# The sums of the tokens' quarters move from GpSimd to VectorE, with a new order of the work

## The chip, the cores and the metric

The kernel runs on one core of a Trainium2 chip. A core has five engines that each work through a queue of their own, in order: TensorE (PE in the profile) for matrix products, VectorE (DVE), ScalarE (ACT), GpSimd (POOL) and SyncE (SP), which here only issues DMAs. Semaphores make one engine wait for another. The metric is the device time of one execution in microseconds; the time of a kernel is the median of several runs.

## The reference

The input `x` has 2048 tokens of width 512. After a layer norm two branches read it, and their product is added to `x`:

```python
x = A_x
xn = _layernorm(x, axis=-1)
s = _A_ref(xn, A_wqkv, A_wo)                   # linear attention, 32 heads of 16
g = _silu(_B_ref(xn, B_w1, B_w2, B_w3, B_w4))  # token shift mixer, then an MLP of width 1376
return x + s * g
```

Branch A projects `xn` to q, k and v and applies `phi(t) = where(t > 0, t + 1, exp(t)) + 1e-6` to q and k. It forms `kv = sum over tokens of phi(k) v` per head and `z = sum of phi(k)`, and gives `phi(q) kv / (phi(q) z + 1e-6)`, times `wo`. Branch B norms its input again, multiplies by `w1`, applies gelu, shifts the four quarters of the channels by +1, -1, +2 and -2 tokens, multiplies by `w2` and adds its input; then it norms, multiplies by `w3`, applies gelu, multiplies by `w4` and adds again. All of it is float32.

## The kernel before

**Precision and products.** Each operand of a large matrix product is split into a rounded part and the rest (`rounded`: ScalarE rounds to the high part, VectorE subtracts it to get the low part). `products` then takes three matmuls for each product: high by high, high by low, low by high. Larger products are done as two by two blocks with seven block products in place of eight (the scheme of Strassen in Winograd's form). `seven` does so for the mixer, the MLP and the attention, `keys_queries` for the projections to keys and queries. The operands of those seven products are sums and differences of blocks.

**Stages.** The tokens go in four blocks of 512. In the first 245 us the kernel does, for each block, the keys and queries, the sums over tokens (`gram`, tile `g`), the first half of the mixer (`mix1`, tile `h`, then `forms`) and the second (`mix2`, tiles `pam`, `pbm`, `pem`, output `o`). From 245 us on it does the MLP and the attention block by block (`up_pair`, `down` into `acc`, `attend_pair`, `gate`).

**The step that the change touches.** Blocks 0 and 1 form keys and queries with plain products. Blocks 2 and 3 use seven products, with forms of the weights made once in `forms_kq` (tiles `kq`, asked for by the item `("T",)` of the list `ORD`) and forms of the tokens made in `make_u`. `make_u(b)` first subtracts the token means from four transposed chunks `xt` (128 channels by 512 tokens each) and rounds these to tiles `u`. Then it makes four sums `us_0` to `us_3` of quarters. With quarters numbered by token half and by channel half, they are `q10+q11`, `us_0-q00`, `q00-q10` and `q01-us_1`. Each is two instructions of 128 by 256 elements, on the engine that `SUMS` names, so eight in each block and sixteen in all. ScalarE and VectorE round them to the left operands `s1` to `s4` of `keys_queries` (products into `pbk`, `pek`, `pak`).

**Banks.** Matmul results go to PSUM, where four banks of 512 columns (pool `mm`) are used in turn beside four accumulators. A bank comes free when VectorE or ScalarE has read it: in `mix1` by the product `ht`, in `mix2` by the additions `o`, in `keys_queries` by `p1k`, `p5k` and `u2k`.

**What sets the order.** The program first lists all 5074 operations. `Plan.emit` then puts them into the engines' queues with a planner that holds an estimate of each operation's time. Every operation has a due time, worked out backward from the matmul that needs it; among those that can go at about the same time, the one due first goes. A tile of the pool `p` (96 buffers) may be opened only a certain time ahead of its due time; `SOON` adds to this time for items of `ORD` ("T" for the forms `kq`, "u" for `make_u`). The table `SOONER` holds pairs: the number of an operation in the list, and by how many quarters of a microsecond its due time is made earlier (later if negative). What an operation reads is made due earlier with it. The planner lets a two-operand operation of VectorE on SBUF wait until one of GpSimd has ended (`port`). Since one plan sets all queues, a changed entry can move instructions and DMAs on SP's and POOL's queues too.

Of the kernel before, what the change touches and what calls it, by code (L numbers as in the profile page):

```python
# [396 lines left out]
def linear_attn_gated_by_mixer(  # L397
# [27 lines left out]
    WARM = 8  # L425
    PIECE = BT + W
    EARLY = (), ()
    SUMS = "POOL"
    SOON = {"T": 24.0, "u": 5.0}
    AHEAD = 70.0, 50.0, 30.0, 10.0, 0.0  # L430
    TH = BT // 2
    EDGE = 64
# [15 lines left out]
    def rounds(name):  # L448

        return piece(name + "h", F32R), piece(name + "l", F32R)  # L450
# [221 lines left out]
    def make_u(b):  # L672
# [12 lines left out]
        for n, u, v, op in ((0, q[1, 0], q[1, 1], ALU.add), (1, parts[0], q[0, 0], ALU.subtract),  # L685
                            (2, q[0, 0], q[1, 0], ALU.subtract), (3, q[0, 1], parts[1], ALU.subtract)):
            for c in range(2):
                pl.tt(parts[n][c], u[c], v[c], op, eng=SUMS)
            hl = rounds(f"us{b}_{n}")
# [702 lines left out]
    for what, *args in ORD:  # L1392
        pl.early = SOON.get(what, 0.0)
        DO[what](*args)
# [48 lines left out]
    for b in range(NQ):  # L1443
# [64 lines left out]
                gate(b * QT + QT - 1, a, o, D // 2, late=True, by_dma=False, whole=o > 0)  # L1508

    SOONER = (  # L1510
        23, 66, 83, 70, 97, 31, 156, 19, 186, 1, 424, 8, 536, 32, 925, -16, 930, -96, 981, 8, 1172, 16, 1530, 32,
        1761, 16, 3072, -16, 4805, 8, 4809, 438,
    )
    pl.emit(first=6.0, lead={"p": 14.0, "w": 14.0, "ab": 10.0}, reserve={"p": 20, "w": 1, "ab": 0}, window=12.0,
            ahead=6.0, table=SOONER)
# [37 lines left out]
```

## Time and profile before

| | us |
|---|---|
| median of 3 runs (lowest to highest) | 524.08 (522.8 to 525.65) |
| the profiled execution | 524.87 |
| its span, first to last instruction | 523.2 |
| TensorE busy in it | 511.5 |
| VectorE busy | 417.0 |
| ScalarE busy | 338.9 |
| GpSimd busy | 117.9 |

The profile records one execution. Busy time is time in which an engine has an instruction running; waiting for a semaphore is not counted, but an instruction that has started and is held up by something else counts as busy for all of that. The span does not contain the 1.67 us by which the execution's time is longer. "Granted clock" is the TensorE clock as a share of full speed. In rows of instructions the columns are the start, the duration, the engine, the line, the operation, and output <- inputs by the names of the program with block and chunk numbers partly left out; brackets hold the idle time before and what ended it. Where a row ends in x2, two instructions are drawn together.

### The profile page before, as it was taken

Reading aid. Unit: us, or ns where it says so; the run is one execution under the profiler, and the core shown is the slowest. Engines: PE = TensorE matmul, PEld = TensorE weight load, DVE = VectorE, ACT = ScalarE, POOL = GpSimd, SP = SyncE. Lnnn points to the kernel's source line nnn. Section 1 sums busy time; section 2 is a strip of 40 time slices with the busy share of each in tenths; the row PEclk is TensorE's granted clock in tenths of the full one; section 3 lists DMA queues with packets and bytes.
Section 4 is the critical chain, followed back from the end, with each engine's and each line's share of the span. In section 5 each row is a group of like instructions: output and inputs, shape, how many; then the busy total and the mean of one; then the engine's idle time right before and its main releaser. Section 6 shows DMA issues by size and latency. Waiting matters only on the chain.

```text
span 523.2 us, 8982 instructions
## 1 busy us (share of the span) xinstructions
PE 511.5 (98%) x2983; PEld 444.3 (85%) x2983; DVE 417.0 (80%) x816; ACT 338.9 (65%) x694; POOL 117.9 (23%) x207
## 2 busy tenths in 40 slices
PE   8999999998999899999999999999999999999996
PEld 6777888897778787898989989899899899999985
DVE  4986669999879996789999988786797758755635
ACT  6898777773899589887777744445453456443621
POOL 3488321246622843111100002000020000200000
PEclk9999999998999899999999999999999999999999
DMA  7987971998598978999976668758687474677504
GB/s 277 302 201 148 273 170 42 240 297 188 177 254 237 225 229 203 302 195 292 333 250 183 206 223 198 230 182 237 199 197 242 163 198 119 159 220 219 204 1 121
DMA packets 78194, 109.05 MB, mean 208 GB/s; under 512 B 8396, under 2 KB 31460, under 8 KB 78148
## 3 DMA queue, kind: packets, MB, share of 16 engines
q1 hardware_dynamic: 68788, 91.44, 54.8%
q0 software_dynamic: 9360, 17.04, 20.1%
q8 instruction: 23, 0.38, 0.3%
q14 instruction: 23, 0.19, 0.1%
HBM read 67.15 MB, written 32.91 MB: 191 GB/s over the span
## 4 chain that ended last, share of the span: by engine, by line
PE 80%; ACT 13%; DVE 3%; issue 2%; DMA 1%; SPq 0%; ACTq 0%; DVEq 0%
PE acc L147 23%; PE pb L147 11%; PE h L147 6%; PE pe L147 6%; PE g L147 5%; PE pbs L147 4%; PE k L147 4%; PE pa L147 3%; PE q L147 3%; PE pbm L147 3%; PE pes L147 2%; PE a L147 2%; PE pbk L147 2%; PE pem L147 1%; ACT qe L168 1%
## 5 line engine op out<-in xcount | busy, mean ns | idle before, releaser
L224 POOL DMA_DIRECT2D th<-in_x x14 | 12.3, 899 | 245.4 <-PE a L147 122.6
L224 POOL DMA_DIRECT2D zacc<-kr x16 | 15.5, 967 | 47.6 <-DVE kr L200 23.1
L168 ACT ACTIVATE p<-pb 128x256 f32<-128x256 f32 x20 | 7.7, 384 | 28.1 <-PE pb L147 27.7
L168 ACT ACTIVATE th<-xo 128x512 f32<-128x512 f32 (+1 forms) x16 | 9.9, 620 | 22.9 <-DVE xo L190 22.6
L224 POOL DMA_DIRECT2D o<-x x16 | 14.5, 907 | 36.5 <-DVE o L190 17.6
L224 POOL DMA_DIRECT2D pqd<-qe x16 | 16.3, 1060 | 23.3 <-ACT ht L168 9.0
L168 ACT ACTIVATE gf<-gf 128x512 f32<-128x512 f32 (+1 forms) x40 | 21.0, 524 | 0.9
L190 DVE TENSOR_TENSOR xo<-acc,xo 128x512 f32<-128x512 f32 (+1 forms) x16 | 10.5, 671 | 12.8 <-PE acc L147 12.8
L190 DVE TENSOR_TENSOR gf<-pa,p 128x256 f32<-128x256 f32 x20 | 8.4, 420 | 14.9 <-PE pa L147 11.6
L168 ACT ACTIVATE p<-pe 128x256 f32<-128x256 f32 x20 | 7.7, 384 | 19.1 <-PE pe L147 19.1
L190 DVE TENSOR_TENSOR gf<-u,pe 128x256 f32<-128x256 f32 x20 | 8.3, 416 | 11.4 <-PE pe L147 11.1
L168 ACT ACTIVATE ht<-ht 128x512 f32<-128x512 f32 x16 | 9.8, 628 | 7.3 <-DVE ht L190 7.2
L190 DVE TENSOR_TENSOR ht<-h,abc 128x512 f32<-128x512 f32 x16 | 10.7, 682 | 4.1 <-PE h L147 3.9
L200 DVE SCALAR_TENSOR_TENSOR kr<-kt,kr 128x512 f32<-128x512 f32 x16 | 10.9, 683 | 3.4 <-ACT kt L168 3.4
L168 ACT ACTIVATE x<-x,nm,rs 128x512 f32<-128x512 f32 x16 | 12.8, 806 | 1.1 <-POOL nm L190 1.1
L168 ACT ACTIVATE y<-o,nm,rs 128x512 f32<-128x512 f32 x16 | 12.0, 806 | 0.9 <-POOL nm L195 0.9
L200 DVE SCALAR_TENSOR_TENSOR qz<-pq,zb 128x512 f32<-128x512 f32 x16 | 10.8, 685 | 0.7 <-DMA pq<-pqd 0.7
L168 ACT ACTIVATE u<-pb 128x256 f32<-128x256 f32 x20 | 7.7, 383 | 5.5 <-PE pb L147 5.5
L200 DVE SCALAR_TENSOR_TENSOR th<-th,so 128x512 f32<-128x512 f32 (+1 forms) x17 | 10.9, 653 | 0.4
L200 DVE SCALAR_TENSOR_TENSOR pq<-pq,rd 128x512 f32<-128x512 f32 x16 | 11.0, 687 | 0.1
L168 ACT ACT_TABLE_LOAD x8 | 10.3, 1283 | 0.9 <-PEq L1544 0.8
L601 POOL TENSOR_TENSOR rs<-w,nhalf 128x4 f32<-128x4 f32 (+2 forms) x10 | 10.6, 1061 | 0.8
(1682 smaller groups left out, 2265.2 us busy)
## 6 DMA issues: line engine op xcount, KB each, us to landing
w_s<-in_w SPq DMA_DIRECT2D x28, 256.0 KB, 5.7
x<-in_x SPq DMA_DIRECT2D x16, 256.0 KB, 3.4
zacc<-kr POOLq DMA_DIRECT2D x16, 256.0 KB, 5.6
pqd<-qr SPq DMA_DIRECT2D x16, 256.0 KB, 4.1
pqd<-qe POOLq DMA_DIRECT2D x16, 256.0 KB, 6.7
o<-x POOLq DMA_DIRECT2D x16, 256.0 KB, 5.6
x1d<-o SPq DMA_DIRECT2D x16, 256.0 KB, 4.1
pq<-pqd SPq DMA_DIRECT2D x16, 256.0 KB, 2.9
```

The costliest lines, as they stand in the source:

```text
L147: lambda: nc.tensor.matmul(out.get(), lhs.get(), rhs.get(), start=start, stop=stop, skip_group_check=more))
L168: nc.scalar.activation(out.get(), src.get(), func, scale=get(scale), **kw)
L190: self.vec(eng, out, [a, b], lambda: self.e(eng).tensor_tensor(out.get(), a.get(), b.get(), op=op), True)
L200: lambda: self.nc.vector.scalar_tensor_tensor(out.get(), a.get(), get(s), b.get(), op0=op0, op1=op1),
L224: lambda: self.nc.gpsimd.dma_start(out.get(), get(src), accum_op=ALU.add), mb=mb)
L601: lambda: g.tensor_tensor(out.get(), src.get(), nh.get(), op=ALU.pow))
```

## The change

The sixteen sums are issued to VectorE in place of GpSimd. The forms `kq` may open their buffers 30 us ahead instead of 24. The table of due times is replaced as a whole. Nothing else differs: the operations and their operands are the same, and blocks 0 and 1, which do not call `make_u`, have no such sums.

```diff
-    SUMS = "POOL"
-    SOON = {"T": 24.0, "u": 5.0}
+    SUMS = "DVE"
+    SOON = {"T": 30.0, "u": 5.0}
...
     SOONER = (
-        23, 66, 83, 70, 97, 31, 156, 19, 186, 1, 424, 8, 536, 32, 925, -16, 930, -96, 981, 8, 1172, 16, 1530, 32,
-        1761, 16, 3072, -16, 4805, 8, 4809, 438,
+        36, 64, 186, 8, 199, 16, 1412, -8, 1489, 8, 1493, 41, 1549, 16, 1982, 4, 2419, -8, 2854, 16, 3165, 8,
+        4113, -8, 4394, -8, 4725, 64, 4805, 16, 4810, 65, 4814, -32,
     )
```

The lines that use the first of these stand in `make_u`:

```python
for n, u, v, op in ((0, q[1, 0], q[1, 1], ALU.add), (1, parts[0], q[0, 0], ALU.subtract),
                    (2, q[0, 0], q[1, 0], ALU.subtract), (3, q[0, 1], parts[1], ALU.subtract)):
    for c in range(2):
        pl.tt(parts[n][c], u[c], v[c], op, eng=SUMS)
```

## The prediction

> **What bounds the kernel now.** I read the page first, then the waits of TensorE, then windows, and then the timeline of the two places which the windows show.
>
> ```profile
> PE 511.5 (98%) x2983; PEld 444.3 (85%) x2983; DVE 417.0 (80%) x816; ACT 338.9 (65%) x694; POOL 117.9 (23%) x207
> PE 80%; ACT 13%; DVE 3%; issue 2%; DMA 1%; SPq 0%; ACTq 0%; DVEq 0%
> ```
>
> TensorE (PE) is busy for 511.5 of 523.2 us, the chain that ends last is 80% PE, and the change touches no matmul. So only two things can move the end: the 11.7 us in which PE is idle, and the time in which it runs at a lower clock. The next rows cut the span into stretches. The columns are the stretch, its length, the busy time with instruction counts of PE, PEld, DVE, ACT and POOL, the granted clock, the DMA share and GB/s (the rows up to 518.50 are of PE alone).
>
> ```profile
> 0.00:40.00 40.00, 37.88 (x146) 1.00 0.88 260
> 190.00:245.00 55.00, 54.66 (x295) 1.00 0.96 242
> 245.00:518.50 273.50, 273.38 (x1817) 1.00 0.67 198
> ...
> 60.00:80.00 20.00, 20.00 (x88) 16.23 (x87) 12.68 (x24) 14.58 (x27) 3.50 (x4) 1.00 0.76 201
> 80.00:130.00 50.00, 47.76 (x279) 41.97 (x278) 49.14 (x97) 33.66 (x66) 18.78 (x27) 0.97 0.77 200
> 130.00:150.00 20.00, 19.98 (x87) 15.82 (x87) 15.39 (x28) 17.41 (x28) 12.67 (x27) 1.00 0.68 187
> 150.00:190.00 40.00, 37.88 (x192) 30.87 (x191) 37.32 (x66) 31.85 (x62) 19.37 (x32) 0.96 0.94 239
> 119.30:121.40 2.10, 0.06 (x1) 0.00 (x0) 2.10 (x3) 1.53 (x3) 2.03 (x3) 1.00 1.00 227
> 121.40:126.30 4.90, 4.86 (x22) 4.50 (x23) 4.71 (x12) 0.22 (x1) 1.49 (x2) 0.65 1.02 258
> 176.50:178.80 2.30, 0.27 (x2) 0.00 (x0) 2.30 (x6) 0.00 (x0) 1.11 (x3) 1.00 1.11 255
> 178.80:183.20 4.40, 4.38 (x15) 3.66 (x16) 4.37 (x7) 0.90 (x2) 4.21 (x11) 0.62 1.00 274
> ```
>
> From 245 us on, PE loses 0.12 us: nothing is to be had there. What it loses in mid-kernel lies at two places, which I call stall A (119.3 us) and stall B (176.5 us). Each has two parts: PE stands still, 2.10 - 0.06 = 2.04 us and 2.30 - 0.27 = 2.03 us, and then its clock is down, which costs (1 - 0.65) x 4.90 = 1.72 us and (1 - 0.62) x 4.40 = 1.67 us. A is 3.76 us, B 3.70 us, together 7.46 us. At both VectorE (DVE) is busy throughout, and the waits of PE say that it is DVE's evacuation of a PSUM bank that ends last:
>
> ```profile
> PE pbk L147 <- DVE o L190: 2.1, 1, 2.1
> PE pbm L147 <- DVE o L190: 2.0, 1, 2.0
> ```
>
> The timeline at A (start, duration, engine, operation; the chunk sums are the rows that write `us`) and at B:
>
> ```profile
> 115.08 1.76 POOL L190 TENSOR_TENSOR us<-xt,xt 128x256 f32<-128x256 f32 x2
> 115.90 0.69 DVE L595 BATCH_NORM_STATS2 st<-xs 128x6 f32<-128x512 f32 x1
> 116.50 0.41 DVE L190 TENSOR_TENSOR o<-pbm,p5m 128x256 f32<-128x256 f32 x1
> 116.91 4.14 DVE L190 TENSOR_TENSOR u_0l<-xt,u_0h 128x512 fp32r<-128x512 f32 x1
> 117.27 1.87 POOL L190 TENSOR_TENSOR us<-us,xt 128x256 f32<-128x256 f32 x2
> 118.67 1.82 POOL L190 TENSOR_TENSOR us<-xt,us 128x256 f32<-128x256 f32 x2
> 120.97 0.41 DVE L190 TENSOR_TENSOR o<-pam,p1m 128x256 f32<-128x256 f32 x1
> ...
> 172.80 2.43 DVE L190 TENSOR_TENSOR u_2l<-xt,u_2h 128x512 fp32r<-128x512 f32 x1
> 173.25 2.56 POOL L190 TENSOR_TENSOR us<-xt,xt 128x256 f32<-128x256 f32 x1
> 173.95 2.99 POOL L190 TENSOR_TENSOR us<-us,xt 128x256 f32<-128x256 f32 x1
> 175.15 1.21 DVE L190 TENSOR_TENSOR u_3l<-xt,u_3h 128x512 fp32r<-128x512 f32 x1
> 176.29 1.21 DVE L190 TENSOR_TENSOR us_2l<-us,us_2h 128x512 fp32r<-128x512 f32 x1
> 178.77 2.27 DVE L190 TENSOR_TENSOR us_0l<-us,us_0h 128x512 fp32r<-128x512 f32 x1
> ...
> 166.33 1.23 DVE L190 TENSOR_TENSOR xt<-xt,um 128x512 f32<-128x512 f32 x1
> 183.30 1.22 DVE L190 TENSOR_TENSOR w_al<-w_s,w_ah 128x512 fp32r<-128x512 f32 x1
> 105.86 0.75 DVE L190 TENSOR_TENSOR hs2f<-hs1f,ht 128x256 f32<-128x256 f32 x1
> ```
>
> The row to see is `u_0l`: 4.14 us, where the same form, undisturbed, takes 0.69 (row `x10l` below). It stands beside the chunk sums on GpSimd (POOL), and the evacuation of `pam`, for which PE waits, stands behind it in DVE's queue. Instructions with one SBUF input (statistics, 0.69) or one PSUM input (`o`, 0.41) run beside the same sums without loss. All stretched rows have two SBUF inputs.
>
> **The change part by part.** (1) Sixteen sums leave POOL. Their price on DVE is that of the same form there, by distance from start to start:
>
> ```profile
> 109.69 0.42 DVE L190 TENSOR_TENSOR hs2f<-hs1f,ht 128x256 f32<-128x256 f32 x1
> 110.02 0.42 DVE L190 TENSOR_TENSOR ha121l<-ht,ha121h 128x256 fp32r<-128x256 f32 x1
> 143.31 0.69 DVE L190 TENSOR_TENSOR x10l<-x,x10h 128x512 fp32r<-128x512 f32 x1 [1.02 <-ACT x10h L168]
> ```
>
> That is 0.33 us of queue each, 8 x 0.33 = 2.6 us per block. (2) In return the stretches go. Against 0.69 (0.42) they are 3.45 and 0.33 us for block 2, and 0.54 + 1.74 + 0.52 + 0.52 + 1.58 + 0.53 = 5.43 us for block 3. So DVE gets 1.2 us less work in block 2 and 2.8 us less in block 3.
>
> Does it fit? In 80:130 DVE needs 49.14 - 3.78 + 2.6 = 48.0 us, and without A the stretch lasts 50 - 3.76 = 46.2 us: 1.8 us too little. In 150:190 it needs 37.32 - 5.43 + 2.6 = 34.5 of 40 - 3.70 = 36.3: it fits. What can leave the first stretch are the four statistics of the rows of block 3, which PE first needs, as transposes of their means and scales, at 135 us:
>
> ```profile
> 135.09 0.11 PE cb L152
> ...
> L595 DVE BATCH_NORM_STATS2 st<-xs 128x6 f32<-128x512 f32 x4 | 2.5, 676 | 0.0
> ...
> 80.00:130.00 50.00, 8.33 (x14) 0.97 0.77 200
> 130.00:135.00 5.00, 1.85 (x3) 1.00 0.11 29
> ```
>
> Their 2.5 us would find room in 130:150, where DVE is busy 15.39 of 20 us. Best case the 1.8 us costs nothing; if all of it stays ahead of evacuations, 1.8 us. I take half, 0.9 us, since the order ranks by due time but the trace shows the statistics ahead of an evacuation (115.90).
>
> (3) `SOON` for "T" from 24 to 30 lets the forms `kq` take buffers up to 6 us sooner. The last two rows above are DVE's `kq` work: 8.33 us before 130 and 1.85 us behind it. Pulled ahead, that 1.85 us would come into the full stretch, unless some moves to 60:80, where DVE has 7.3 us free. Bounds 0 to 1.85 us; I take 0, because the due times behind them stay and 6 us only permits an earlier start.
>
> (4) The new table. Counted in the order in which the program adds operations, entries 36, 186 and 199 act in the first 40 us, 1412 to 1549 on blocks 2 and 3 (1549 is a sum of block 3), 1982 to 4394 on the second half, 4725 to 4814 on the end. Dropped with the old one are the pulls on `x1h` (83) and `k2h` (156); 36 takes the place of 23, since pulling an operation also pulls what it reads. The start holds these waits:
>
> ```profile
> 5.49 2.04 PE L147 MATMUL k<-wk_s,xt 128*128 128x512 f32 x2 [0.66 <-DMA wk_s<-in_wqkv]
> 35.38 1.20 PE L147 MATMUL g<-k2h,x2h 128*128 128x512 f32 x4 [0.33 <-ACT k2h L168]
> ```
>
> So the start can win at most about 1 us, and without the pulls it can lose as much; no row speaks for one side, and I take 0. Behind 245 us PE's own queue covers the entries: 0, with 0.12 us to win. Every pull also reorders loads on SP and accumulating DMAs on POOL. I allow 0.4 us for all this, the gap in 190:245 (55.00 - 54.66 = 0.34) being what one such stretch loses under this planner.
>
> (5) POOL is left with its DMA issues and small operations. Accumulations `o<-x` queued among the sums go out sooner. What waits for those is statistics and stores, not PE: 0 us, and no cover is lost. ScalarE (ACT), which rounds the sums, now waits for DVE; a pair takes 0.33 + 0.42 = 0.75 us there against 1.76 to 1.87 on POOL. Queued behind each sum on DVE are evacuations of PSUM banks; one sum holds them up for 0.33 us, which the cover at A (below) takes.
>
> What a rest of a stall costs is open: at both places a wait of about 2.03 us was enough to lower the clock, and none below 1 us shows it. [...]
>
> The sum: -7.46 (A and B) + 0.9 + 0.4 = -6.2 us. The profiled execution took 524.87 us (span 523.2 and 1.67 around it), so 518.7; the median of the runs, 524.08, is 0.8 lower, so I predict 518.0.
>
> **The rivals.** *DVE becomes the bound (slower).* Place: 80 to 130 us. If the forms come into the full stretch too, and the statistics stay, DVE is 1.8 + 1.85 = 3.65 us short, and each short piece stands ahead of an evacuation. It decides where more than 2.1 us of queue stands ahead of one: the 4.14 us of `u_0l` made PE wait 2.04, so 2.1 is covered. Two waits with their cold clocks cost 3.65 + 2 x 1.7 = 7.1 us against the 3.76 removed, +3.3; B is then counted as unchanged, the late queue delaying it too. Median 524.1 + 3.3 = 527.4. For it speaks DVE at 49.14 of 50; against it, that DVE's total falls in both stretches. [...]
>
> *Only one stall goes.* B's demand fits, A's does not: -3.7 + 0.4 gives 520.8. For it: the 1.8 us shortage. *The change is not felt:* the stretches end, but the new order makes two stalls of like size elsewhere, or the stretches are not due to the sums and stay. The `hs2f` at 105.86 loses only 0.33 us beside two sums, which speaks for the second. It gives 524; with none of the sums' 5.3 us covered it would be 529.4.
>
> **How the numbers follow.** Both stalls gone 0.48 (range 515.5 to 520.5); one gone 0.16; no difference 0.12; DVE the bound 0.24. Half a per cent, 2.6 us, is about what a measurement can tell here. One stall gone, 520.8, is still over it, but only just, and I count three quarters as faster: 0.48 + 0.12 = 0.60. Same is 0.04 + 0.12 = 0.16, slower 0.24. Cases of both signs hold much of the chance, so the range runs from 515.5 (both gone, start better) to 528.5 (bound, start 1 us worse).
>
> **What would show it.** Right: sixteen `us` rows on DVE at about 0.42, none on POOL; no two-input DVE row of 512 columns above 0.8 us between 100 and 190; clock 1.00 in both stretches, PE idle there under 1 us. Step 2 fails if stretched rows stay; the half of 1.8 us fails if PE waits for `o`, `p1k` or `ht` near 105 to 130. A clock below 1.00 in a new place, or a start that loses over 3 us, would make the forecast wrong.

## The result and the profile after

The changed kernel takes 517.61 us (median of 4 runs, 517.36 to 518.14) against 524.87 us for the kernel before, on the same chip (four runs, the three of its table above and one more). The ratio is 0.9868, with a 95% interval of 0.9835 to 0.9902. That is 7.3 us, and the prediction was 518.0 us with a range of 515.5 to 528.5. The profiled execution took 517.69 us with a span of 515.8 us, 7.4 us less than the span before.

The page of the changed kernel, first the busy times, then the granted clock in 40 slices:

```profile
PE 507.6 (98%) x2983; PEld 441.1 (86%) x2983; DVE 412.4 (80%) x832; ACT 337.9 (66%) x694; POOL 104.6 (20%) x191
PEclk9999999999999999999999999999999999999999
```

The number of matmuls is the same. VectorE has sixteen instructions more and GpSimd sixteen fewer, and yet VectorE is busy 4.6 us less. No slice has a lowered clock any more.

The windows of the changed kernel by stage (columns: stretch, length, busy time and count of PE, PEld, DVE, ACT and POOL, granted clock, DMA share, GB/s):

```profile
0.00:40.00 40.00, 38.22 (x152) 29.02 (x153) 31.65 (x66) 32.91 (x63) 20.58 (x51) 1.00 0.83 258
40.00:100.00 60.00, 59.78 (x280) 48.46 (x279) 47.64 (x88) 47.97 (x84) 22.17 (x43) 1.00 0.75 175
100.00:130.00 30.00, 29.71 (x189) 26.61 (x188) 29.48 (x63) 20.42 (x43) 11.53 (x22) 1.00 0.90 247
130.00:160.00 30.00, 29.03 (x128) 22.40 (x127) 24.97 (x58) 26.51 (x48) 10.63 (x18) 1.00 0.79 234
160.00:190.00 30.00, 30.00 (x167) 25.86 (x166) 29.69 (x63) 27.20 (x51) 15.62 (x29) 1.00 0.96 250
190.00:245.00 55.00, 54.80 (x318) 46.47 (x317) 46.24 (x94) 46.28 (x98) 9.65 (x11) 1.00 1.01 263
245.00:511.00 266.00, 266.00 (x1761) 242.25 (x1759) 201.41 (x403) 136.24 (x312) 14.42 (x18) 1.00 0.66 193
```

The windows of the kernel before that the prediction did not show (here PE is the only engine):

```profile
40.00:100.00 60.00, 60.00 (x282) 1.00 0.72 169
100.00:130.00 30.00, 27.76 (x173) 0.94 0.91 246
130.00:160.00 30.00, 29.94 (x128) 1.00 0.78 219
160.00:190.00 30.00, 27.92 (x151) 0.94 0.93 225
```

PE's loss in a stretch is counted here as its idle time plus, where the clock is down, the missing share of the clock times the length:

| stretch, us | before: idle + clock | after | difference |
|---|---|---|---|
| 0 to 40 | 2.12 | 1.78 | -0.34 |
| 40 to 100 | 0.00 | 0.22 | +0.22 |
| 100 to 130 | 2.24 + 1.80 | 0.29 | -3.75 |
| 130 to 160 | 0.06 | 0.97 | +0.91 |
| 160 to 190 | 2.08 + 1.80 | 0.00 | -3.88 |
| 190 to 245 | 0.34 | 0.20 | -0.14 |
| 245 to the end of PE's work | 0.12 | 0.00 | -0.12 |

The sum is -7.1 of the 7.4 us. Both stalls are gone with their slow clocks, and 0.9 us is lost in a new place, 130 to 160 us. What is left of PE's waits there and elsewhere is short (total, number, longest):

```profile
PE pbk L147 <- DVE ht L190: 0.5, 1, 0.5
PE pbk L147 <- ACT p1k L168: 0.4, 1, 0.4
PE pbm L147 <- DVE o L190: 0.3, 1, 0.3
```

The place of stall A in the timeline of the changed kernel:

```profile
114.05 0.69 DVE L190 TENSOR_TENSOR u_0l<-xt,u_0h 128x512 fp32r<-128x512 f32 x1
114.98 0.75 DVE L190 TENSOR_TENSOR us<-xt,xt 128x256 f32<-128x256 f32 x2
116.66 0.42 DVE L190 TENSOR_TENSOR o<-pam,p1m 128x256 f32<-128x256 f32 x1
```

`u_0l` takes 0.69 us where it took 4.14, a pair of sums takes 0.75 us on VectorE, and the evacuation of `pam` comes in time. Of the stretched rows nothing is left between 100 and 190 us.

### The profile page after: what moved, and what is told of

Its sections match the earlier page's. It is cut to its first block, busy times and chain, and to the rows that moved or that the text cites. A ratio compares the mean times of both kernels' runs of the same rounds, so it can differ in the third digit from the quotient of the medians.

```text
span 515.8 us, 8950 instructions
## 1 busy us (share of the span) xinstructions
PE 507.6 (98%) x2983; PEld 441.1 (86%) x2983; DVE 412.4 (80%) x832; ACT 337.9 (66%) x694; POOL 104.6 (20%) x191
## 4 chain that ended last, share of the span: by engine, by line
PE 77%; ACT 14%; DVE 3%; DMA 2%; issue 2%; POOL 1%; SPq 0%; ACTq 0%; DVEq 0%; POOLq 0%
PE acc L147 23%; PE pb L147 11%; PE pe L147 6%; PE pbs L147 4%; PE h L147 4%; PE g L147 4%; PE k L147 3%; PE pbm L147 3%; PE pa L147 3%; PE pes L147 2%; PE a L147 2%; ACT qe L168 2%; PE pbk L147 2%; PE q L147 2%; DMA o<-x 2%
## 5 line engine op out<-in xcount | busy, mean ns | idle before, releaser
L224 POOL DMA_DIRECT2D pqd<-qe x16 | 14.8, 927 | 20.4 <-DMA pqd<-qr 8.8
```

Source lines behind the costliest of these rows:

```text
L224: lambda: self.nc.gpsimd.dma_start(out.get(), get(src), accum_op=ALU.add), mb=mb)
```

## The experiments

Two theories were to be told apart first. The port theory, named after the planner's `port`: two-operand sums on GpSimd hold up two-operand work of VectorE on SBUF, and PE waits behind that. That it is a port by which they do so, no run shows. The order theory: the new table and the longer lead bring the gain. Times of one paragraph are from one chip, and each run has the kernel before beside it.

### The engine alone, planned anew

In the kernel before:

```diff
-    SUMS = "POOL"
+    SUMS = "DVE"
```

> The kernel before with the sums on VectorE; lead of the forms and table stay the old ones, the planner orders anew by itself. Port theory (two-input sums on GpSimd hold up two-input work on VectorE, and PE waits behind it): no stretched rows, both clock drops gone, 517 to 521 us. Order theory (the new table and lead bring the gain, the engine does not): 522 to 527 us, with stalls left that the old table does not cure.

Measured: 517.75 us against 523.76, ratio 0.9899 (0.9862 to 0.9935). The old table and lead give the gain once the engine is changed: the ratio of the whole change, 0.9868 (0.9835 to 0.9902), cannot be told from this one. No row of VectorE is stretched between 100 and 190 us. Its profiled execution was the slowest of five, 521.78 us, the others 517.24 to 518.34. It shows a stall that the others, 3.4 us faster and more, can hardly have in that size, and so one clock drop that the port theory did not expect. The waits of PE, the instruction of ScalarE that stood ahead of the evacuation, and the window behind:

```profile
PE pem L147 <- ACT p5m L168: 2.4, 2, 1.7
...
121.37 0.63 ACT L168 ACTIVATE x8h<-x 128x512 fp32r<-128x512 f32 x1 [2.09 <-DMA o<-x]
...
122.00:126.50 4.50, 4.18 (x17) 3.79 (x18) 2.70 (x7) 1.06 (x4) 1.28 (x2) 0.62 1.05 295
```

ScalarE waited 2.09 us for an accumulating DMA of GpSimd's queue before it could write `x8h`; behind it in its queue stood `p5m`, for which PE waited 1.7 us, and the clock went down. The most likely link is a buffer: the DMA reads a tile `x`, and the new tile takes such a buffer over. This was read from the waits, not tried.

### The new order alone, sums on GpSimd

In the changed kernel:

```diff
-    SUMS = "DVE"
+    SUMS = "POOL"
```

> The changed kernel with the sums planned and issued on GpSimd again; new lead and new table. Port theory: two-input rows on VectorE beside the sums are stretched by 5 us or more in total, at least one clock drop, 522 to 528 us. Order theory: 516 to 520 us.

Measured: 530.56 us, ratio 1.0115 (1.0080 to 1.0151), slower than the kernel before and than either theory had it. The stretches came to 5 us. But the largest loss is one that neither named (PE's waits, and the chain ahead of it):

```profile
PE pbk L147 <- DVE ht L190: 7.3, 1, 7.3
...
151.18 5.86 DMA abc<-arow
157.16 0.70 DVE ht L190
```

The load of the scales `abc` for block 3 was issued so late on SP that `ht`, and with it a PSUM bank, came 7.3 us late. In the 15 us ahead of that load the chain runs through ScalarE, one unstretched row of VectorE and the loads and stores of SP, so this is a fault of the order and not of the port. The new table and lead are worth nothing by themselves for sums on GpSimd; planned so, it is 6.8 us slower than the kernel before.

### Either order to the instruction, only the engine of the sums exchanged

The sums are planned for the engine that `SUMS` names and issued on the other one; this is the changed kernel, and the kernel before has `nc.vector` in this place.

```diff
-                pl.tt(parts[n][c], u[c], v[c], op, eng=SUMS)
+                pl.vec(SUMS, parts[n][c], [u[c], v[c]], lambda o=parts[n][c], p=u[c], q=v[c], op=op:
+                       nc.gpsimd.tensor_tensor(o.get(), p.get(), q.get(), op=op), True)
```

The changed kernel's order with the sums on GpSimd:

> The changed kernel's plan, to the instruction, with only the engine that runs the sixteen sums set back to GpSimd. Port theory: stretches of 5 to 10 us in total come back around 115 to 125 and 165 to 177 us, PE stalls of about 2 us with a clock drop behind, 522 to 527 us. Order theory: 517 to 519 us, as the order is the same. A third theory, that the sums' own slowness on GpSimd (about 0.9 us against 0.33) makes the left operands late: waits of PE fall on matmuls that read us, not on evacuations.

The order of the kernel before with the sums on VectorE:

> The plan of the kernel before, to the instruction, with only the engine of the sixteen sums set to VectorE. Port theory: stretches gone, both stalls under 1 us, 516 to 520 us. Order theory: 523 to 526 us. VectorE-is-full theory: 525 us or more, since 5.3 us are added to a queue that was planned without them.

Measured on the same chip: 529.31 us (ratio 1.0103, 1.0072 to 1.0135) and 517.82 us (0.9886, 0.9859 to 0.9912). With the old order kept, the engine alone brings 5.9 us, with the new order kept nearly 12 us (529.31 against the changed kernel's 517.61, from another set of runs). The first one is 2 us slower than even the port theory had it, and its stretches come to 11.3 us. Its windows, waits of PE and two of its ten stretched rows:

```profile
100.00:130.00 30.00, 27.48 (x172) 24.62 (x171) 29.14 (x48) 18.34 (x40) 17.07 (x30) 0.94 0.94 255
160.00:190.00 30.00, 25.62 (x146) 21.96 (x145) 27.56 (x46) 24.29 (x47) 17.94 (x32) 0.94 0.84 205
...
PE pbk L147 <- ACT p1k L168: 4.7, 2, 4.3
PE pbm L147 <- DVE o L190: 1.8, 1, 1.8
...
116.70 3.42 DVE L190 TENSOR_TENSOR u_1l<-xt,u_1h 128x512 fp32r<-128x512 f32 x1
178.74 1.78 DVE L190 TENSOR_TENSOR us_1l<-us,us_1h 128x512 fp32r<-128x512 f32 x1 [1.07 <-ACT us_1h L168]
```

And the second one's:

```profile
100.00:130.00 30.00, 29.38 (x186) 25.94 (x185) 29.79 (x71) 20.18 (x42) 11.89 (x16) 1.00 0.92 249
160.00:190.00 30.00, 29.77 (x168) 25.26 (x167) 27.95 (x61) 25.35 (x49) 14.76 (x27) 1.00 0.95 241
...
PE pbm L147 <- DVE o L190: 0.4, 2, 0.3
```

In the old order no stretched row is left in this stretch, PE waits 0.4 us for `o`, and the clock stays up. The order theory and the theory that VectorE is full have fallen. The wait of 4.3 us on ScalarE in the other shows that the stretch is not all that sums on GpSimd cost: ScalarE itself waited for late sums there, 1.20, 1.90 and 1.35 us one after the other, before it came to `p1k`. That left a third theory, that their slowness does the harm.

### Added work on GpSimd that nobody waits for

In the changed kernel, behind each sum on VectorE, one of three kinds of work is issued on GpSimd. It goes to the tile `ones`, which the start alone uses.

```diff
 nc.vector.tensor_tensor(o.get(), p.get(), q.get(), op=op)
+for k in (0, P):
+    nc.gpsimd.tensor_tensor(ones.all.get(), p.get()[:, k:k + P], q.get()[:, k:k + P], op=op)
```

```diff
+for k in (0, P):
+    nc.gpsimd.tensor_scalar(ones.all.get(), p.get()[:, k:k + P], 1.0, None, op0=ALU.mult)
```

```diff
+nc.gpsimd.tensor_copy(ones[:, :4].get(), p.get()[:, :4])
+for k in range(4):
+    nc.gpsimd.memset(ones.all.get(), 0.0)
```

> The changed kernel, and beside each of the sixteen sums on VectorE GpSimd makes the same sum once more, in two halves of 128 columns, into a tile that nobody reads. So no left operand can be late because of GpSimd. Port theory: two-input rows on VectorE are stretched by 4 us or more in total and the time is 520 to 527 us. Late-operand theory (the sums were only slow on GpSimd): no stretched rows, 517 to 519 us.

> As before, but the added work on GpSimd reads one tile (a multiplication by 1), also in two halves. If any read of SBUF by GpSimd holds up two-input work on VectorE: stretches of 2 us or more, 519 to 524 us. If only two-input work on GpSimd does: no stretches, 517 to 519 us.

> As before, but the added work on GpSimd only writes (four memsets of 128 columns behind a copy of 4 columns which waits for the same operand). If reads are what counts: under 1 us of stretches, 517 to 519 us. If GpSimd's mere activity counts: as with the added sums.

Measured on one chip: 523.81 us with two inputs, 523.72 with one, 520.83 with writes only, where the kernel before has 524.21. The stretches sort as the port theory has it, the times do not. With two inputs VectorE's rows are stretched by about 6.5 us in total; with one input by about 1.3 us, in fourteen rows of at most 0.16 us each; with writes by none. Two rows of the first kind and one of the second:

```profile
116.29 0.95 DVE L190 TENSOR_TENSOR u_1l<-xt,u_1h 128x512 fp32r<-128x512 f32 x1
117.16 0.68 DVE L689 TENSOR_TENSOR us<-us,xt 128x256 f32<-128x256 f32 x1
...
117.40 0.77 DVE L190 TENSOR_TENSOR u_1l<-xt,u_1h 128x512 fp32r<-128x512 f32 x1
```

The first two lose 0.26 us each beside halves of 128 columns, the third 0.08 us. So reads of one tile do hold VectorE up, but little; neither of the two outcomes put down for them (2 us or more, and none) came. Yet the second kind loses as much time as the first. Who waited for its added work (total, number):

```profile
  ACT u2k L168: 3.5, 1
  ACT us_3h L168: 2.1, 1
  ACT p1k L168: 1.6, 1
```

`u2k` and `p1k` evacuate banks and read nothing of the added work. What they can have waited for is buffers which its late reads of `xt` and `us` still held; this is read from the waits and the program, not tried. The premise that nobody waits was wrong, so these three don't price the port. They point to a second way from GpSimd to PE: its lateness holds buffers of the pool `p`, ScalarE stops at a tile it cannot open, and the evacuations stand behind.

### The sums made copies of one operand, in the old kernel

```diff
-                pl.tt(parts[n][c], u[c], v[c], op, eng=SUMS)
+                r = (v, u, u, v)[n][c]
+                pl.vec(SUMS, parts[n][c], [u[c], v[c]], lambda o=parts[n][c], r=r:
+                       nc.gpsimd.tensor_scalar(o.get(), r.get(), 1.0, None, op0=ALU.mult), True)
```

> The kernel before, its plan, engine and waits, with each of the sixteen sums turned into a copy of one of its two operands (the later one): GpSimd reads one tile, so the sums are left out and the left operands hold other values. The added one-input work of the earlier run stretched nothing on VectorE. Port theory: no stretched rows, the waits for the evacuations at 119 and 176 us gone, 516 to 520 us. If it is GpSimd's slowness or its hold on buffers that makes the stalls: both stay, 522 to 526 us.

Measured: 516.83 us against 524.27, ratio 0.9860 (0.9834 to 0.9886). Engine, order and the late operand are those of the kernel before; only one input is missing, and with it the sums, so the output is another. The timeline at stall A (the last row of these three holds four instructions), at the `hs2f` that lost 0.33 us in the kernel before, and at stall B, then the windows:

```profile
116.12 0.66 DVE L190 TENSOR_TENSOR u_0l<-xt,u_0h 128x512 fp32r<-128x512 f32 x1
116.70 0.42 DVE L190 TENSOR_TENSOR o<-pam,p1m 128x256 f32<-128x256 f32 x1
116.73 3.77 POOL L689 TENSOR_SCALAR us<-us 128x256 f32<-128x256 f32 x4
...
105.10 1.72 POOL L689 TENSOR_SCALAR us<-xt 128x256 f32<-128x256 f32 x2 [4.83 <-DVE xt L190]
105.40 0.42 DVE L190 TENSOR_TENSOR hs2f<-hs1f,ht 128x256 f32<-128x256 f32 x1
...
167.14 2.39 POOL L689 TENSOR_SCALAR us<-xt 128x256 f32<-128x256 f32 x1
168.13 0.68 DVE L190 TENSOR_TENSOR u_2l<-xt,u_2h 128x512 fp32r<-128x512 f32 x1
168.73 1.04 DVE L190 TENSOR_TENSOR u_3l<-xt,u_3h 128x512 fp32r<-128x512 f32 x1
...
100.00:130.00 30.00, 30.00 (x191) 27.09 (x190) 28.96 (x65) 20.96 (x43) 18.45 (x31) 1.00 0.91 242
160.00:190.00 30.00, 29.85 (x159) 24.63 (x159) 27.57 (x54) 25.26 (x49) 21.97 (x36) 1.00 0.96 232
```

`u_0l` is back at 0.66 us, both stalls and both clock drops are gone, although GpSimd was no faster: its copies took 0.85 to 2.62 us, and ScalarE waited 2.9 us for them in total, where it had waited 0.2 us for the sums. Beside the copies `hs2f` takes 0.42 us (0.75 before), `u_2l` 0.68 (2.43) and `u_3l` 1.04 (1.21). Stretched rows were to be gone; five are left between 100 and 190 us, of 0.16 to 0.35 us each and 1.1 us together, where the sums had cost 9.2 us. (That the added one-input work stretched nothing, as the expectation has it, is not what its run shows: 1.3 us in fourteen rows, as above.)

At stall A the comparison is weaker than it looks. One pair of copies ends at 116.31 us, the next starts at 116.73, and `u_0l` runs from 116.12 to 116.78, so it hardly meets them; in the kernel before a pair of sums started in the middle of it. So in the kernel before it was the sums with two inputs that stalled PE, by way of VectorE's stretched rows, and not their slowness. That the second input does it is shown by `hs2f`, by stall B and by the added work above; for `u_0l` alone it is inferred.

### What the table and the lead are worth on VectorE

Three variants of the changed kernel: the lead back at 24, an empty table, and the lead at 24 with a mixed table.

```diff
-    SOON = {"T": 30.0, "u": 5.0}
+    SOON = {"T": 24.0, "u": 5.0}
```

```diff
-            ahead=6.0, table=SOONER)
+            ahead=6.0, table=())
```

```diff
-        36, 64, 186, 8, 199, 16, 1412, -8, 1489, 8, 1493, 41, 1549, 16, 1982, 4, 2419, -8, 2854, 16, 3165, 8,
-        4113, -8, 4394, -8, 4725, 64, 4805, 16, 4810, 65, 4814, -32,
+        36, 64, 186, 8, 199, 16, 424, 8, 536, 32, 925, -16, 930, -96, 981, 8, 1172, 16, 1530, 32,
+        1761, 16, 3072, -16, 4805, 8, 4809, 438,
```

> The changed kernel with the lead of the forms back at 24. My step 3 (the lead costs and brings nothing): 517 to 518.5 us. If the earlier forms make room in the full stretch: 518.5 us or more, with PE waits between 100 and 130 us.

> The changed kernel with an empty table. If the table carries part of the gain on VectorE: 520 us or more. If the planner with VectorE sums does by itself what is needed: 517 to 519 us.

> Sums on VectorE, lead of the forms 24 as before, and a table of the new entries for the first 40 us with the old entries for the rest. Order-matters theory: the changed kernel's start loses about 1.4 us less than the old one, and the old rest loses less between 130 and 180 us, so 516 to 517.3 us, faster than the changed kernel. Order-does-not-matter theory: 517.3 to 518.5 us.

> The changed kernel as it is, on the same chip as the three others, to compare them with it: 517 to 518.2 us.

Measured on one chip: 517.24 us for the changed kernel, 517.07 with the lead at 24, 520.86 with no table, 523.92 with the mixed one (eleven runs of 521.03 to 526.10, and one of 529.63). The lead does nothing that can be measured. A table is worth 3.6 us here, but the old one, made for sums on GpSimd, serves as well as the new within what can be measured (517.75 and 517.82 above, on another chip; ratios 0.9899 and 0.9886 against 0.9867 here). The mixed table was to be the fastest and loses the whole gain, without one stretched row. PE's waits and the chain ahead of the first one:

```profile
PE pbk L147 <- DVE ht L190: 3.2, 1, 3.2
PE pbk L147 <- DVE p5k L190: 1.4, 1, 1.4
...
145.86 5.99 DMA abc<-arow
151.98 0.70 DVE ht L190
```

It is the late load of `abc` again, and the clock behind the first wait falls too, to 0.94 over 130 to 160 us. Against the kernel with the engine alone, this table differs only in entries of the first 40 us; the planner carried that through to 150 us.

## Why the prediction was right

**What bounds the kernel.** Right. The two stalls were the thing to win: 3.75 and 3.88 us went, against 3.76 and 3.70 forecast. That the times lie within 0.4 us is in part luck: the gain was put at 6.2 us and came to 7.3, but the forecast started from 524.08 us for the kernel before, which then came to 524.87. (The steps of the sum give 517.9, not 518.0.)

**Steps 1 and 2, sums and stretches.** Right. The sums cost 0.33 us each in VectorE's queue, the stretches between 100 and 190 us went, and VectorE's busy time fell by 4.6 us where 4.0 was worked out. What in the chip holds the rows up, the runs do not show. They show that the size hung on GpSimd's inputs: beside two-input sums 0.69 us became up to 4.14 (the kernel before), beside one-input work no row lost over 0.35 us (the copies), and beside writes alone none lost anything.

**Does it fit.** Too careful. I left half of 1.8 us in stall A; PE is idle for 0.29 us in all of 100 to 130, with VectorE busy 29.48 of 30 us. The four statistics that I had called movable did move behind the place of stall A, to between 127.2 and 130.2 us. But that was not needed: the old order with the sums on VectorE kept them ahead, from 116.1 us on, and PE lost 0.62 us there with VectorE busy 29.79 of 30 us. So a full engine did not matter in either order; why its work comes out in time I did not test.

**Step 3, the lead.** Right at 0: 517.07 and 517.24 us.

**Step 4, the table.** 0.4 us allowed; the stretches outside the stalls changed by -0.34 + 0.22 + 0.91 - 0.14 - 0.12 = +0.5 us. The size was right and the reason half so. I treated the table as small pulls at the places of its entries. The runs show 3.6 us between table and no table, and about 5 us lost at 150 us by entries for the first 40 us (3.2 us of waiting, and 1.8 us by the lowered clock). A new order could have taken the gain away, and my range held that only under another name.

**Step 5, GpSimd's queue.** Wrong as a claim, without effect on the sum. I said that what waits for its accumulations is statistics and stores, not PE. The slowest execution of the engine-alone kernel shows ScalarE stopped for 2.09 us by one, with PE behind. The runs with one-input and write-only work added are 6.5 and 3.6 us slower than the changed kernel on their chip (517.24), with stretches of 1.3 us and of none.

**The rivals.** VectorE as the bound fell with 517.82 us in an order planned without the sums. One stall gone, and no effect, did not occur. The sign of "not felt", the `hs2f` that lost only 0.33 us, misled: sums and two-input work side by side do not always cost the whole overlap, but the second input is the cause all the same.

## What to carry to other kernels

Look in the trace for rows that are several times longer than the same form elsewhere, and for what another engine does beside them. Here VectorE was "busy" in such a row and mostly held up (4.14 us for work of 0.69), so moving two-input work from GpSimd to a VectorE that was busy for 49.14 of the 50 us from 80 to 130 made VectorE's whole load smaller (417.0 us before, 412.4 after). Separate engine and order by exchanging the engine inside a fixed order: it took two runs and settled what two planned variants could not. And before calling GpSimd's work off the path, ask which buffers its reads hold and who opens them next.

## What the runs showed of the hardware

In these runs the longer waits of PE cost more than their length, the shorter ones did not. Waits of 1.7 us (`pem`, the engine-alone run) and of 2.0 us (both stalls before) were followed by a clock of 0.62 to 0.65 on average over 4.4 to 4.9 us, which by the missing share of the clock is about 1.7 us each time. Behind the waits of 1.8 and 4.3 us (the changed kernel's order with the sums on GpSimd) the clock fell too: it was 0.94 over 100 to 130 and over 160 to 190 us, again 1.8 us each. Behind a wait of 1.4 us (`p5k`, mixed table) it stayed at 1.00 over 186 to 196 us, and behind those of 1.5 and 1.6 us (`u2k` and `p1k`, one-input work) at 1.00 over 160 to 190 and 190 to 245 us. Whether the length alone decides between 1.6 and 1.7 us, these runs do not show.
